# A planner's price for a step of attention is raised, and chunks of the last two batches have one tile each

## The chip, the cores and the metric

The kernel runs on one core of a Trainium2 chip. The metric is the device time of one execution in microseconds (us), as the median of several runs. The core has a matrix engine (TensorE; PE in the profile, PEld for its weight loads), VectorE (DVE), ScalarE (ACT), GpSimd (POOL) and a queue for transfers (SyncE, SP). Each engine works off its own list of instructions in order.

## The reference, cut to what matters

```python
# q, k, v: (batch 8, heads 8, sequence 576, head_dim 64), float32
scores = scale * np.matmul(q, k.transpose(0, 1, 3, 2))
kth = np.partition(scores, -32, axis=-1)[..., -32:-31]     # the 32nd largest of a row
scores = np.where(scores >= kth, scores, -1e9)
attn = softmax(scores)                                      # exp(s - max) / (sum + 1e-9)
x = np.matmul(attn, v)                                      # then (B*S, H*D) = (4608, 512)

h = x @ w_in                                                # w_in: (512, 2048)
g = np.where(h >= 1, h, np.where(h <= -1, 0, (h + 1) ** 2 / 4))
out = g @ w_out                                             # w_out: (2048, 512)
```

Attention keeps only the 32 largest scores of each row, and a feed-forward block (the MLP) follows on the same tokens.

## The kernel before, in words

**Steps of attention.** A batch's 576 queries are cut into four tiles of 128 and a tail of 64. The tails of two batches share one tile of tokens. A step takes one tile of queries for two heads (or half of a tail's heads); there are 144 steps, numbered from 0. In a step TensorE multiplies queries and keys (`scores`, L269), ScalarE copies the scores to `s` (L271), VectorE finds the 32 largest of each row by rounds of eight (L279 to L324: maximum of pairs, maxima, replacement) and masks the exponentials (L330), its reciprocal of their sum is L336, GpSimd normalizes (L343), and the weights are transposed, either by TensorE (`transpose_w`, L357) or, in most steps, through DRAM (`move_w`: a ScalarE copy at L372 and two transfers). Then TensorE multiplies the weights and the values (`values`, L389), and ScalarE copies the result into `xT` (L402), which holds the tokens for the MLP.

**The MLP.** It works on chunks of one or two tiles of 128 tokens. For each of 16 blocks of the hidden layer, `hidden` makes four matmuls into `ph` (L419) over all columns of the chunk at once; ScalarE forms `r` and `g` from it (L423, L431), and GpSimd finishes `g` (L436 to L438). `final` multiplies `g` by `w_out` into `py` (L444), one tile at a time, four blocks behind `hidden` (`LAG = 4`). `ph` has two buffers, shared with the values of attention. So a pair of tiles shares the weight loads of L419 and the instructions on ScalarE and GpSimd, while a single tile can start as soon as that tile's attention is done. A unit in the planner is a 128-column part of this work; a tile has 64 units of `hidden` and 64 of `final`.

**What sets the order.** The order on the four compute engines is written out while the program is built (`manual_schedule`). Each step is walked in seven slots; after each slot `advance` hands out MLP products that are ready. It keeps two model clocks. `dve_time` is VectorE's: a step adds `K_TIME`, and `PIECE_TIME` for each piece of weights that is converted in it. `pe_time` is TensorE's: scores add 1.15, values 1.25, a unit of MLP work `UNIT_TIME` = 0.218. A product is handed out only while `pe_time` is below the slot's time `now` on VectorE's clock, and only while its share `due` of the remaining work lasts. What is left after the last step is worked off at the end. `K_TIME` thus says how long a step is, and so how much MLP work fits beside it. `chunks` (L462 to L470) says which tiles go together: single tiles in the first two batches, pairs after that, and in the last two batches two pairs, the shared tail, and four single tiles.

The start, in which weights are converted from 64-bit words (`early`), lasts for the first steps; the change doesn't touch it.

Of the kernel before, what the change touches and what calls it, by code (L numbers as in the profile page):

```python
# [24 lines left out]
def kernel(  # L25
# [131 lines left out]
    def run(ctx, paired):  # L157
# [304 lines left out]
        rounds, chunks = [], []  # L462
        for b in range(0, B, 2):
            a, c, tl = [(b, t) for t in range(NT)], [(b + 1, t) for t in range(NT)], (b, NT)
            if b + 2 < B:
                rounds += a + [tl] + c + [(b + 1, NT)]
                chunks += [a[0:2], a[2:4], c[0:2], c[2:4], [tl]] if b else [[x] for x in a + c + [tl]]
            else:
                rounds += a + [tl, (b + 1, NT)] + c
                chunks += [a[0:2], a[2:4], [tl]] + [[x] for x in c]  # L470
        steps = []
        for b, t in rounds:
            tile_of = (b, t) if t < NT else (b - b % 2, t)
# [36 lines left out]
                inspected += 1  # L510


        K_TIME, PIECE_TIME, UNIT_TIME, SLOTS, EARLY_STEPS, EARLY_SHARE = 10.2, 0.55, 0.218, 7, 4, 32
        pe_time, dve_time, done, scored, ready_at, usable = 9.0, 12.0, {}, {}, {}, {0: 0.0}

        def advance(amount, until):
# [172 lines left out]
    with ExitStack() as inner:  # L689
        run(inner, True)  # L690
    again = nc.values_load(flag[0:1, 0:1], min_val=0, max_val=1)
    with tc.If(again > 0):
        with ExitStack() as inner:
            run(inner, False)
# [27 lines left out]
```

## Time and profile before

The time is 1684.64 us (median of 3 runs, 1683.96 to 1685.89); the profiled execution took 1683.5 us.

| engine | busy us | share of the span |
|---|---|---|
| PE | 1549.2 | 92% |
| PEld | 1050.8 | 62% |
| DVE | 1550.5 | 92% |
| ACT | 1188.2 | 71% |
| POOL | 974.8 | 58% |

The costliest groups are the output products (L444, 564.3 us busy) and the hidden products (L419, 594.1 us) on TensorE, and the replacement and maxima (L306, 375.6 us; L315, 348.9 us) on VectorE. Busy shares are means over the whole span, so they are to be read together with the rows by slice, which show when an engine was busy. TensorE's busy time counts a matmul from its start to a modelled end, and matmuls overlap. A row of the timeline or of the groups names the line, the engine, the operation, what is written and what is read, and in brackets the idle time before and what ended it.

### The profile page before, as it was taken

Reading aid. Unit: us, or ns where it says so; the run is one execution under the profiler, and the core shown is the slowest. Engines: PE = TensorE matmul, PEld = TensorE weight load, DVE = VectorE, ACT = ScalarE, POOL = GpSimd, SP = SyncE. Lnnn points to the kernel's source line nnn. Section 1 sums busy time; section 2 is a strip of 40 time slices with the busy share of each in tenths; the row PEclk is TensorE's granted clock in tenths of the full one; section 3 lists DMA queues with packets and bytes.
Section 4 is the critical chain, followed back from the end, with each engine's and each line's share of the span. In section 5 each row is a group of like instructions: output and inputs, shape, how many; then the busy total and the mean of one; then the engine's idle time right before and its main releaser. Section 6 shows DMA issues by size and latency. Waiting matters only on the chain.

```text
span 1683.5 us, 30910 instructions
## 1 busy us (share of the span) xinstructions
PE 1549.2 (92%) x9645; PEld 1050.8 (62%) x9645; DVE 1550.5 (92%) x4875; ACT 1188.2 (71%) x2552; POOL 974.8 (58%) x1720
## 2 busy tenths in 40 slices
PE   5586999999998899979999999979999999999998
PEld 4464666666665666646566766646566666666675
DVE  6999999999999999999999999999999999999922
ACT  5677677777777767777677877767667877767743
POOL 4675677666665554536465755526465765657750
PEclk6698999999998999979999999979999999999999
DMA  9333345455555546554555555554555544544400
GB/s 246 114 98 91 86 132 160 129 151 141 140 154 156 144 135 174 142 157 135 146 159 143 150 142 151 158 158 124 155 150 151 143 131 130 132 133 117 114 27 16
DMA packets 439055, 227.83 MB, mean 135 GB/s; under 512 B 393056, under 2 KB 401248, under 8 KB 438880
## 3 DMA queue, kind: packets, MB, share of 16 engines
q1 hardware_dynamic: 438880, 225.75, 49.4%
q8 instruction: 78, 1.28, 0.3%
q14 instruction: 97, 0.79, 0.2%
HBM read 62.91 MB, written 86.11 MB: 89 GB/s over the span
## 4 chain that ended last, share of the span: by engine, by line
DVE 51%; PE 33%; ACT 7%; issue 3%; POOL 3%; DMA 2%; SPq 1%; DVEq 0%; POOLq 0%; ACTq 0%
PE ph L419 13%; DVE more L306 12%; PE py L444 12%; DVE tops L315 10%; DVE e L330 8%; DVE more L317 4%; DVE seconds L320 4%; DVE tops L290 4%; DVE more L279 4%; PE po L389 3%; PE sp L269 3%; ACT halves L372 2%; ACT e L293 1%; DVE z L335 1%; DVE kth L324 1%
## 5 line engine op out<-in xcount | busy, mean ns | idle before, releaser
L419 PEld LDWEIGHTS ph<-xT,w_in 128*128 128x128 f32 x3328 | 505.1, 195 | 199.0 <-issue 88.5
L419 PE MATMUL ph<-xT,w_in 128*128 128x128 f32 (+1 forms) x3328 | 594.1, 326 | 32.8 <-ACT g L431 18.6
L444 PE MATMUL py<-w_out,g 128*128 128x512 f32 x1152 | 564.3, 605 | 2.0 <-POOL w_out L136 1.8
L423 ACT ACTIVATE r<-ph,half 128x128 f32<-128x128 f32 (+1 forms) x416 | 169.7, 408 | 292.9 <-PE ph L419 237.6
L306 DVE MATCH_REPLACE8 more<-tops,more 128x288 f32<-128x288 f32 x864 | 375.6, 442 | 0.0
L436 POOL TENSOR_SCALAR r<-r 128x128 f32<-128x128 f32 (+1 forms) x392 | 164.9, 421 | 343.4 <-ACT r L423 342.1
L315 DVE MAX8 tops<-more 128x8 f32<-128x288 f32 x864 | 348.9, 445 | 0.0
L343 POOL TENSOR_SCALAR e<-e,rz 128x576 f32<-128x576 f32 x260 | 211.9, 825 | 205.2 <-DVE rz L336 205.2
L372 ACT COPY halves<-e 128x1152 uint16<-128x1152 uint16 x260 | 286.9, 1156 | 14.7 <-POOL e L343 14.0
L444 PEld LDWEIGHTS py<-w_out,g 128*128 128x128 f32 x1152 | 197.4, 191 | 145.9 <-issue 117.8
L438 POOL TENSOR_TENSOR g<-r,g 128x128 f32<-128x128 f32 (+1 forms) x400 | 261.6, 654 | 31.4
L330 DVE SCALAR_TENSOR_TENSOR e<-s,kth,e 128x576 f32<-128x576 f32 x288 | 242.0, 877 | 0.5
L437 POOL TENSOR_TENSOR r<-r 128x128 f32<-128x128 f32 (+1 forms) x392 | 219.0, 559 | 32.7
L293 ACT ACTIVATE e<-s,nmax 128x576 f32<-128x576 f32 x288 | 218.4, 771 | 4.8
L269 PE MATMUL sp<-kT,qT 64*128 64x288 f32 x1024 | 169.0, 447 | 9.9 <-ACT kT L229 9.1
L271 ACT ACTIVATE s<-sp 128x576 f32<-128x576 f32 x288 | 170.0, 642 | 6.6 <-PE sp L269 6.4
L389 PE MATMUL po<-wT,v_in 128*64 128x128 f32 x2048 | 148.5, 287 | 22.1 <-DMA wT<-rows 13.9
L389 PEld LDWEIGHTS po<-wT,v_in 128*64 128x64 f32 x2048 | 115.5, 141 | 80.7 <-issue 18.3
L431 ACT ACTIVATE g<-ph,minus 128x128 f32<-128x128 f32 (+1 forms) x400 | 162.4, 406 | 0.0
L269 PEld LDWEIGHTS sp<-kT,qT 64*128 64x128 f32 x1024 | 91.8, 193 | 84.6 <-issue 40.6
L320 DVE MAX8 seconds<-more 128x8 f32<-128x288 f32 x288 | 118.3, 452 | 13.9
L317 DVE TENSOR_TENSOR more<-s 128x576 f32<-128x576 f32 x144 | 122.4, 850 | 4.9
(88 smaller groups left out, 1349.6 us busy)
## 6 DMA issues: line engine op xcount, KB each, us to landing
rows<-halves SPq DMA_DIRECT2D x130, 576.0 KB, 2.8
raw<-in_moe_w_out_dram SPq DMA_DIRECT2D x52, 256.0 KB, 3.0
raw<-in_moe_w_in_dram SPq DMA_DIRECT2D x48, 256.0 KB, 3.1
k_in<-in_k_dram SPq DMA_DIRECT2D x64, 128.0 KB, 2.9
q_in<-in_q_dram SPq DMA_DIRECT2D x32, 256.0 KB, 3.1
v_in<-in_v_dram SPq DMA_DIRECT2D x8, 1024.0 KB, 6.0
out_dram<-y SPq DMA_DIRECT2D x32, 256.0 KB, 2.6
kT<-in_moe_w_in_dram SPq DMA_DIRECT2D x16, 256.0 KB, 4.5
```

What stands on the lines that cost most here:

```text
L269: nc.tensor.matmul(o[:, a0 - c0:a1 - c0], qT[d, g, :], kT[d, g, k0:k0 + a1 - a0], start=True, stop=True)
L293: nc.scalar.activation(e[:, i, :], s[:, i, :], AF.Exp, bias=nmax[:, i:i + 1])
L306: nc.vector.match_replace(out=rest[:, i, :], in_to_replace=tops[:, i, r - 8:r], in_values=src[:, i, :], imm_value=LOWEST)
L315: nc.vector.max(out=tops[:, i, r:r + 8], in_=src[:, i, :])
L330: nc.vector.scalar_tensor_tensor(out=e[:, i, :], in0=s[:, i, :], scalar=last[:, i:i + 1], in1=e[:, i, :], op0=ALU.is_ge, op1=ALU.mult, acc ...
L343: nc.gpsimd.tensor_scalar(e[:, i, :], e[:, i, :], rz[:, i:i + 1], 1.0, ALU.mult, ALU.mult)
L372: nc.scalar.copy(halves[:, :, i * S:(i + 1) * S], st["e"][:, i, :].bitcast(U16).rearrange("p (k t) -> p t k", t=2))
L389: nc.tensor.matmul(po[j * D:(j + 1) * D], v_in[:, h, c, :] if c < NT else v_tl[0][:, h, :], wT[:, block(j, c)], start=(c == 0), stop=(c == ...
L419: nc.tensor.matmul(ph, w_in[:, kk, f * P:(f + 1) * P], xT[:, kk, c0:c1], start=(kk == 0), stop=(kk == NK - 1))
L437: nc.gpsimd.tensor_tensor(out=r, in0=r, in1=r, op=ALU.mult)
L438: nc.gpsimd.tensor_tensor(out=g, in0=r, in1=g, op=ALU.add)
L444: nc.tensor.matmul(pys[i], gs[f][:, i * P:(i + 1) * P], w_out[:, f, :], start=(f == 0), stop=(f == NF - 1))
```

## The change

`K_TIME` goes from 10.2 to 10.7 us, so that the planner takes an attention step to be longer and hands out more MLP products beside each. In the last two batches each chunk has one tile, so that a tile's MLP can begin without waiting for a second tile. The work that is computed is the same.

```diff
@@ -467,7 +467,7 @@
                 chunks += [a[0:2], a[2:4], c[0:2], c[2:4], [tl]] if b else [[x] for x in a + c + [tl]]
             else:
                 rounds += a + [tl, (b + 1, NT)] + c
-                chunks += [a[0:2], a[2:4], [tl]] + [[x] for x in c]
+                chunks += [[x] for x in a + [tl] + c]
         steps = []
         for b, t in rounds:
             tile_of = (b, t) if t < NT else (b - b % 2, t)
@@ -510,7 +510,7 @@
-        K_TIME, PIECE_TIME, UNIT_TIME, SLOTS, EARLY_STEPS, EARLY_SHARE = 10.2, 0.55, 0.218, 7, 4, 32
+        K_TIME, PIECE_TIME, UNIT_TIME, SLOTS, EARLY_STEPS, EARLY_SHARE = 10.7, 0.55, 0.218, 7, 4, 32
         pe_time, dve_time, done, scored, ready_at, usable = 9.0, 12.0, {}, {}, {}, {0: 0.0}
```

## The prediction

> **What bounds the kernel now.** I read the slices of the span first, then the chain, then the busy time by stretch.
>
> ```profile
> PE   5586999999998899979999999979999999999998
> DVE  6999999999999999999999999999999999999922
> PEclk6698999999998999979999999979999999999999
> ...
> DVE 51%; PE 33%; ACT 7%; issue 3%; POOL 3%; DMA 2%; SPq 1%; DVEq 0%; POOLq 0%; ACTq 0%
> ```
>
> VectorE works at 9 tenths until the last two slices, some 80 us in which TensorE alone works off MLP products; TensorE is at 9 tenths nearly everywhere, and the chain hops between the two. So two engines are full, and a "free" 80 us tail must be read against that. The next answer gives busy time by stretch from the end of step 107 (1219 us) on; a row is its window, then its length, then PE, PEld, DVE, ACT, POOL busy, clock, DMA share, GB/s.
>
> ```profile
> 1219.00:1489.00 270.00, 269.21 (x1646) 179.00 (x1645) 262.29 (x828) 197.46 (x399) 162.72 (x268) 0.99 0.52 141
> 1489.00:1542.00 53.00, 48.38 (x312) 34.33 (x310) 51.49 (x163) 37.01 (x83) 33.81 (x69) 0.94 0.41 115
> 1542.00:1607.00 65.00, 64.17 (x458) 45.84 (x460) 61.98 (x194) 47.28 (x115) 48.00 (x101) 1.00 0.41 114
> 1607.00:1684.00 77.00, 69.16 (x417) 49.45 (x411) 10.99 (x40) 26.70 (x81) 20.55 (x55) 0.97 0.04 12
> ```
>
> TensorE idles 0.8, 4.6 and 0.8 us of these 388 us. Since busy time can hide stalls, I priced TensorE's blocks from its timeline, start to start of the next block, at the first quartile of each kind: one-tile hidden product of four matmuls 0.89 us, two-tile one 1.73, output product 0.86, scores of a step 2 x 0.58, values of a step 1.24, a query or key transposition 0.44. The tail shows two of them bare (1642.35 to 1643.21 and to 1644.10):
>
> ```profile
> 1642.35 1.02 PE L444 MATMUL py<-w_out,g 128*128 128x512 f32 x2
> 1643.21 1.05 PE L419 MATMUL ph<-xT,w_in 128*128 128x128 f32 x8
> 1644.10 4.46 PE L444 MATMUL py<-w_out,g 128*128 128x512 f32 x10
> ```
>
> Priced so, 1219 to 1489 holds 260.4 us of work in 270.4 (lost 10.1), 1489 to 1542 holds 42.5 in 53.3 (lost 10.9), 1542 to 1607.5 holds 64.2 in 65.5 (lost 1.3), and the tail to TensorE's last matmul at 1677 holds 66.4 in 67.6 (lost 1.1). In all 433.5 us of work and 23.4 lost; then 6.5 us for the last copy and store. **Everything this change can win after step 107 lies in those 23.4 us.** Part of the loss is VectorE's pace: the second half of a step's scores (L271) lands 4.8 to 6 us before the maximum of pairs (L279) takes it in most steps from 112 to 135. After step 136 this lead is 0.0 to 2.3 us: there TensorE sets the pace already. At the start of a one-tile chunk the loss is of another kind:
>
> ```profile
> 1538.38 2.99 PE L419 MATMUL ph<-xT,w_in 128*128 128x128 f32 x24
> 1542.84 1.16 PE L419 MATMUL ph<-xT,w_in 128*128 128x128 f32 x8 [1.46 <-ACT g L431]
> ```
>
> Hidden products without output products between them (LAG is 4) wait for ScalarE to empty `ph`, which has two buffers.
>
> **What the Trainium skill says.** "Perfetto Trace Analysis", section Identifying the Most-Contended Engine, says that matmul busy share doesn't tell how close TensorE is to its limit; the trace agrees (323 to 456 us: 127 us busy by the profile, 120.1 us of priced work), hence my pricing. "VectorE: DVE Perf Modes", section on the TRN2 errata, gives a ScalarE instruction from PSUM a fixed part of 172 cycles plus one per element at 1.2 GHz: 250 and 357 ns for 128 and 256 columns. The trace has 367 and 473 (L423): the slope agrees, the fixed part is 117 ns larger, and the measurement counts. So halving a chunk pays the fixed part twice. "TensorE: Matmul & The Clock Gate", section What's actually happening, says that after an idle window of about 3.4 us the array runs at half clock. The trace agrees: after gaps of 2.13 and 0.95 us near 1497 us the clock is halved from 1498.7 to 1505.5 us (16 records in 3.78 us, against 1.95 at 1490).
>
> **The change, part by part.** The planner runs while the program is built, so its bookkeeping for both kernels can be counted. A unit is a 128-column quarter of a tile's hidden or output product; a tile has 128.
>
> *K_TIME 10.7.* VectorE's real step is 10.36 us at best and 10.8 on the mean after step 107; so the model now lets TensorE's model clock run 0.5 us further, some 2 units a step. Until step 77 the count at the ends of steps is equal, but for 4 to 16 units early in steps 11 to 22, where `due` or missing tiles bind instead. After step 107 both have 3080 handed out; at the last step before has 4340 and after 4420. The tail's backlog falls from 268 to 188 units: 80 x 0.2188 us (an eighth of 0.89 + 0.86) = 17.5 us less tail. But these 80 units aren't gone. They are put into steps 108 to 143, ahead of scores and values in TensorE's queue. What waits behind them is scores L269, then ScalarE L271, then VectorE L279. The lead of 4.8 us absorbs the first units; after that VectorE pays. With 37.4 units a step in place of 35, priced work is 37.4 x 0.2188 + 1.16 + 1.24 = 10.6 us, plus 0.2 for transpositions: 10.8, before any loss. TensorE becomes the bound of all of these steps, so the end follows from its work and its loss.
>
> *One-tile chunks.* Two pairs become four tiles. TensorE: 32 x (2 x 0.891 - 1.727) = 1.8 us more. The rows by shape:
>
> ```profile
> L423 ACT ACTIVATE r<-ph,half 128x128 f32<-128x128 f32 x256 | 94.0, 367 | 140.7 <-PE ph L419 85.7 <-POOL g L438 41.2 <-POOL r L437 5.9
> L431 ACT ACTIVATE g<-ph,minus 128x128 f32<-128x128 f32 x240 | 87.4, 364 | 0.0
> L423 ACT ACTIVATE r<-ph,half 128x256 f32<-128x256 f32 x160 | 75.6, 473 | 152.2 <-PE ph L419 151.9
> L431 ACT ACTIVATE g<-ph,minus 128x256 f32<-128x256 f32 x160 | 75.0, 469 | 0.0
> ```
>
> ScalarE: 32 x (2 x 731 - 942) ns = 16.6 us more. GpSimd, likewise from L436 to L438 (383 + 457 + 544 against 476 + 706 + 819 ns): 24.5 us more. Both lie beside other work, as ScalarE has 27% idle from 1219 to 1489 and GpSimd 40%. What isn't beside other work is the start of a chunk: nine one-tile chunks now begin between steps 113 and 143, where there were four and two pairs. Starts cost TensorE 0.8, 2.4, 0.8 and 1.7 us late (near 1297, 1494, 1524, 1540 us) and about 2.4, 2.3 and 1.8 us early (359, 403, 452). Bounds 0.8 and 2.4; I take 1.45, the mean of the late four: 13 us. Between starts the one-tile stretches lose 2% (1542 to 1607) up to 5% (323 to 456, less its starts); I take 2.5% of about 320 us: 8. The pair stretch to step 113 keeps its 2, and the tail its 1.1. Sum 24.1 us lost on 435.3 of work, against 23.4 on 433.5: +2.5 us. The gain of readiness (no dry spell near step 124) is in that: with 10.7 and pairs alone the planner would leave 204, with both 188.
>
> *Steps 78 to 97.* Of the same backlog up to 24 more units are out by step 88 (2544 against 2520), yet both run dry at 2816 at step 97. The lead at steps 81 to 86 is 0.0 to 2.1 us already; 12 to 24 units are 2.6 to 5.2 us, so VectorE is delayed by 1 to 4 us. It works back to back afterwards and can't make it up: +3.
>
> *Steps 11 to 22.* Up to 16 units come earlier while TensorE still idles (90 of 113 us busy from 78 to 191): 0 to 2 us gained, I take 1.
>
> Sum: +2.5 + 3 - 1 = +4.5 us, or 1689 us.
>
> **The rivals.** *A, the forecast: TensorE bound, the tail's gain spent in the steps, 1689.* *B: the backlog pays.* If TensorE, never short of work, loses only the 2 to 2.5% of its best stretch, 435.3 x 0.025 = 11 us are lost, 12 fewer than now; against 1.8 for the smaller products and 2 for steps 78 to 97: 1676. For it: that stretch is fed as all steps will be (lag of 12 units, no lead, 38 units a step in 11.2 us). Against it: it is 65 us long, with one start, no key transpositions. *C: no change, 1684.6:* gains of feeding (9 us less from the waits and half clock near 1497) and the new starts cancel. *D: one-tile chunks are as bad as early.* From 323 to 456 us, also one-tile and without lead, 13.4 of 133.5 us are lost; 10% over 320 us is 32, plus 4 elsewhere: 36 against 23.4, plus 1.8 and 3: 1702. Against it: its chunks come just in time, and hidden products wait for `xT` (0.47 us near 360); with a backlog of over 40 units they don't.
>
> **How the numbers follow.** A 0.44, B 0.27, C 0.19, D 0.10. A's bounds (starts at 0.8 or at 2.4 us) run from 1683 to 1698, so a little of it falls within 0.2%, balanced by C's spread. The range from 1674 to 1700 takes in B's centre and leaves out about 2 in 10, most of D and the best of B. Faster by over 0.2% is B: 0.27; within it 0.22; slower 0.51.
>
> **What would show it.** VectorE's last reciprocal (L336), now 1607.5 us, should come near 1629, with 17 us less after it; the mean step from 107 on should grow from 10.8 to about 11.3 us, with VectorE's idle before L279 (10.7 us in all now) at 20 or more; ScalarE's x128 row (L423) should grow by 64, its mean unchanged; hidden products should wait more for ScalarE's `g` L431 (45.9 us on weight loads now). If the steps stay at 10.8 us while the tail shrinks by 17, B is right and my loss at chunk starts is wrong; if idle before L279 stays under 12 us the claim that TensorE becomes the bound falls. If the delay shows already at step 97, the part on steps 78 to 97 is right.

## The result, and the profile after

The changed kernel takes 1700.53 us (median of 4 runs), the kernel before 1684.39 us: ratio 1.0091, 95% interval 1.0074 to 1.0109. It is slower by 16 us, where the prediction had 4.5 us; that is the very end of its range (1674 to 1700 us).

The slices of the span of the changed kernel:

```profile
PE   5586999999998999979899999979999999999998
DVE  6999999999999999999999999999999988899852
PEclk6698999999998999979999999979999999999999
```

Its chain of waits, by engine:

```profile
PE 51%; DVE 33%; ACT 8%; POOL 4%; issue 3%; DMA 1%; SPq 0%; POOLq 0%; DVEq 0%; ACTq 0%
```

VectorE, at 9 tenths up to the tail before, now shows eights in slices 33 to 35 and 38, and works on into slice 39. The chain has changed hands, from 51% on VectorE to 51% on TensorE. The next two lines are the stretch from VectorE's reciprocal of step 107 to its last one, and the tail, in the columns of the prediction:

```profile
1224.50:1635.70 411.20, 399.70 (x2734) 277.12 (x2733) 376.02 (x1185) 296.73 (x675) 286.91 (x557) 0.99 0.47 127
1635.70:1698.60 62.90, 55.75 (x354) 39.91 (x352) 10.79 (x37) 21.50 (x63) 11.31 (x30) 0.99 0.03 11
```

The tail has shrunk, from 76.0 to 62.9 us. But the 36 steps ahead of it have grown from 388.5 to 411.2 us, while VectorE is busy in them for 376 us, as before. Where VectorE waits is told by the idle time before the maximum of pairs:

```profile
L279 DVE TENSOR_TENSOR more<-s 128x576 f32<-128x576 f32 x144 | 113.8, 790 | 32.6 <-ACT s L271 32.5
```

It was 10.7 us in the whole span before, and 1.2 us of that came after step 107; now 24.0 us come after step 107. This accounts for the whole growth of these steps: 22.8 us more idle for 22.7 us. The lead of the scores shows the same: before, the second half of a step's scores was in `s` 4.8 to 6 us ahead of the maximum of pairs in most steps from 112 to 135; now the lead is 0.0 to 1.5 us in every step from 115 on. The longest of these waits is this one, in step 140 (the timeline of VectorE):

```profile
1592.19 0.44 DVE L306 MATCH_REPLACE8 more<-tops,more 128x288 f32<-128x288 f32 x1
1598.31 0.76 DVE L279 TENSOR_TENSOR more<-s 128x576 f32<-128x576 f32 x1 [5.68 <-ACT s L271]
```

And this is TensorE meanwhile, at the start of a one-tile chunk. The first two lines are the row of five hidden products (eight records each) with which a chunk begins:

```profile
1581.92 3.99 PE L419 MATMUL ph<-xT,w_in 128*128 128x128 f32 x32
1586.14 1.16 PE L419 MATMUL ph<-xT,w_in 128*128 128x128 f32 x8 [0.23 <-ACT g L431]
1587.14 1.02 PE L444 MATMUL py<-w_out,g 128*128 128x512 f32 x2
1590.11 1.34 PE L419 MATMUL ph<-xT,w_in 128*128 128x128 f32 x8 [1.95 <-ACT g L431]
1591.25 1.91 PE L444 MATMUL py<-w_out,g 128*128 128x512 f32 x2
1592.95 1.73 PE L419 MATMUL ph<-xT,w_in 128*128 128x128 f32 x8
1594.61 1.24 PE L269 MATMUL sp<-kT,qT 64*128 64x288 f32 x8
```

A hidden product waits 1.95 us for ScalarE to empty `ph`; the scores that VectorE needs stand behind it in TensorE's list. The gap costs more than its length: the granted clock is halved from 1590.95 to 1594.36 us, and the hidden product at 1592.95 takes 1.73 us instead of 1.05. The waits of ScalarE in the same microseconds lead one engine further:

```profile
1585.46 0.37 ACT L423 ACTIVATE r<-ph,half 128x128 f32<-128x128 f32 x1 [0.77 <-POOL g L438]
...
1589.43 0.37 ACT L423 ACTIVATE r<-ph,half 128x128 f32<-128x128 f32 x1 [3.34 <-POOL g L438]
```

ScalarE has no buffer of `r` until GpSimd has finished an earlier block (`r` has two), and GpSimd stood at its normalization (L343) and what follows; some of its instructions were slow there too (L436 took 0.86 us at 1587.5, 0.29 us at 1590.7), for which no run gives the cause. So the chain of this longest wait is GpSimd, `r`, ScalarE, `ph`, TensorE, scores, VectorE.

### The profile page after: what moved, and what is told of

It is laid out like the page before. It is cut to its first block, busy times and chain, and to the rows that moved or that the text cites. A ratio compares the mean times of both kernels' runs of the same rounds, so it can differ in the third digit from the quotient of the medians.

```text
span 1698.6 us, 31644 instructions
## 1 busy us (share of the span) xinstructions
PE 1557.9 (92%) x9901; PEld 1060.4 (62%) x9901; DVE 1557.0 (92%) x4875; ACT 1198.3 (71%) x2616; POOL 1015.4 (60%) x1816
## 4 chain that ended last, share of the span: by engine, by line
PE 51%; DVE 33%; ACT 8%; POOL 4%; issue 3%; DMA 1%; SPq 0%; POOLq 0%; DVEq 0%; ACTq 0%
PE ph L419 19%; PE py L444 19%; DVE more L306 8%; DVE tops L315 7%; PE sp L269 5%; DVE e L330 5%; PE po L389 5%; DVE more L317 3%; DVE seconds L320 3%; DVE tops L290 2%; DVE more L279 2%; ACT halves L372 2%; ACT e L293 1%; POOL g L438 1%; DVE bits L132 1%
## 5 line engine op out<-in xcount | busy, mean ns | idle before, releaser
L419 PEld LDWEIGHTS ph<-xT,w_in 128*128 128x128 f32 x3584 | 519.0, 194 | 205.6 <-issue 95.9
L419 PE MATMUL ph<-xT,w_in 128*128 128x128 f32 (+1 forms) x3584 | 601.5, 314 | 36.9 <-ACT g L431 25.9
L436 POOL TENSOR_SCALAR r<-r 128x128 f32<-128x128 f32 (+1 forms) x424 | 175.8, 415 | 373.4 <-ACT r L423 372.7
L423 ACT ACTIVATE r<-ph,half 128x128 f32<-128x128 f32 (+1 forms) x448 | 178.2, 398 | 296.2 <-PE ph L419 248.0
L343 POOL TENSOR_SCALAR e<-e,rz 128x576 f32<-128x576 f32 x260 | 223.6, 871 | 146.8 <-DVE rz L336 146.8
L437 POOL TENSOR_TENSOR r<-r 128x128 f32<-128x128 f32 (+1 forms) x424 | 231.8, 547 | 35.4
L431 ACT ACTIVATE g<-ph,minus 128x128 f32<-128x128 f32 (+1 forms) x432 | 171.1, 396 | 0.0
L279 DVE TENSOR_TENSOR more<-s 128x576 f32<-128x576 f32 x144 | 113.8, 790 | 32.6 <-ACT s L271 32.5
```

What stands on the lines that cost most here:

```text
L343: nc.gpsimd.tensor_scalar(e[:, i, :], e[:, i, :], rz[:, i:i + 1], 1.0, ALU.mult, ALU.mult)
L419: nc.tensor.matmul(ph, w_in[:, kk, f * P:(f + 1) * P], xT[:, kk, c0:c1], start=(kk == 0), stop=(kk == NK - 1))
L437: nc.gpsimd.tensor_tensor(out=r, in0=r, in1=r, op=ALU.mult)
```

## The experiments

All ratios are to the kernel before on the same chip; the times in us come from several chips, so small differences are to be read from the ratios.

| kernel | us | ratio, 95% interval |
|---|---|---|
| changed kernel | 1700.5 | 1.0091 (1.0074 to 1.0109) |
| 10.7, old chunks | 1689.5 | 1.0044 (1.0025 to 1.0062) |
| 10.2, one-tile chunks | 1688.3 | 1.0026 (1.0019 to 1.0033) |
| 10.7 from step 107, old chunks | 1686.9 | 1.0014 (1.0005 to 1.0023) |
| changed, turns from step 107 | 1684.3 | 1.0000 (0.9990 to 1.0009) |
| changed, turns in all steps | 1675.0 | 0.9949 (0.9933 to 0.9966) |
| before, turns in all steps | 1671.8 | 0.9925 (0.9899 to 0.9950) |
| 10.2, one-tile chunks, turns in all steps | 1671.0 | 0.9923 (0.9906 to 0.9939) |
| 10.7 from step 107, old chunks, turns in all steps | 1668.8 | 0.9916 (0.9891 to 0.9940) |
| changed, `ph` in halves | 1766.7 | 1.0510 (1.0477 to 1.0542) |
| changed, `ph` and `r` in halves | 1750.7 | 1.0398 (1.0369 to 1.0427) |
| changed, LAG 2 | 1723.6 | 1.0237 (1.0220 to 1.0254) |
| changed, LAG 6 | 1739.3 | 1.0333 (1.0316 to 1.0350) |

**The two parts alone.** One run has `K_TIME` 10.7 with the old chunks, one the new chunks with 10.2.

> K_TIME 10.7 with the old chunks. Theory (TensorE bound; delays from two places): VectorE's last reciprocal of step 107 is 5.5 us later than in the kernel before, as in the changed kernel, and the steps after it lose little more, since the pairs stay: 1686 to 1692 us. Rival 1 (more work per step is the whole harm, the chunks none): 1698 or more. Rival 2 (the chunks are the whole harm): 1684 or less.

> One-tile chunks with K_TIME 10.2. Theory: nothing moves up to step 107; after it 1.8 us more work on TensorE and starts of chunks that cost some 1.5 us each, five more of them: 1689 to 1695 us. Rival 1 (work per step is the whole harm): 1684.4. Rival 2 (the chunks are the whole harm): 1698 or more.

Both parts harm, neither is the whole of it: +0.44% and +0.26%. Both single-cause rivals fall. 1689.5 us is within what was expected of 10.7; 1688.3 us is just under the range expected of the chunks. The sum, 0.70%, is below the 0.91% of both together; with intervals of up to 0.18% on either side that difference may be chance. In the profiles the idle before L279 after step 107 is 1.2 us in the kernel before, 8.5 us with 10.7 alone, 4.5 us with the chunks alone, and 24.0 us with both. The leads of the scores suggest why: with 10.2 most steps leave TensorE time to make up for a start, with 10.7 they don't.

**When the longer step costs.**

```diff
-                dve_time = start + K_TIME + PIECE_TIME * min(len(now_converting), n_pieces - converted)
+                dve_time = start + K_TIME + (0.5 if m >= 107 else 0.0) + PIECE_TIME * min(len(now_converting), n_pieces - converted)
```

> Old chunks, and 10.7 only from step 107 on. Theory: the 5.5 us of delay at step 107 are not there, and the rest is as with 10.7 throughout: 5 to 6 us under that run, 1681 to 1687 us. Rival (the harm of 10.7 lies in the steps after 107): within 1.5 us of that run.

1686.9 us is at the upper end of what was expected. It is 2.6 us under 10.7 throughout by the medians and 0.30%, some 5 us, by the ratios, whose intervals just part (1.0023 and 1.0025): a delay before step 107 is there, and is worth a sixth to a third of the whole loss. It can be seen between the reciprocals of steps 77 and 107: 321.4, 321.0 and 321.0 us in the three kernels with 10.2 there (the one before, new chunks alone, 10.7 late), and 326.1, 325.5 and 323.6 in those with 10.7 (the changed kernel, 10.7 alone, the turns below). The last three have the same order of work up to there, so what they differ by is chance.

But VectorE hardly waits for TensorE in these steps. Between the reciprocals of steps 77 and 97 its idle before L279 grows by 0.6 us only, while its own instructions take 3.8 us longer. The stretch before and after (columns as in the prediction; VectorE is the third engine, GpSimd the fifth):

```profile
897.80:1112.70 214.90, 210.28 (x1256) 138.54 (x1254) 208.34 (x660) 161.89 (x329) 121.91 (x207) 0.99 0.57 154
898.60:1118.00 219.40, 212.69 (x1256) 138.24 (x1254) 212.18 (x662) 161.79 (x329) 127.44 (x207) 0.99 0.55 149
```

VectorE is busy for 207.5 to 208.5 us there in all six kernels of the table with 10.2 in these steps. It is busy for 210.4 to 212.2 us in four with 10.7: the changed kernel, 10.7 with the old chunks, and the changed kernel with either kind of turns. The longer ones are L279, L317, L321 and L335 (L335, on two columns, 4.56 us in all before and 6.05 after); on GpSimd L343 and L345 lengthen in the same steps (30.5 to 33.6 and 4.4 to 6.5 us). So the planner's hand-out shifts which instructions of VectorE and GpSimd run beside each other; that they slow each other would fit, but no run isolates it.

What is left of 10.7 after step 107, 0.14%, is the shorter tail (59.1 us from the last reciprocal to the end of TensorE's work, 69.5 before) against longer steps (400.6 us, 388.5 before; 9 us of that is idle before L279 and 3 us longer instructions of VectorE): even with pairs the handed-out work was paid for in full.

**Turns: a start without a row of hidden products.** The last four output products of a chunk alternate with the first four hidden products of the next. Nothing is left out or computed differently, only the order changes.

```diff
-                    pending.extend(mlp(xTs[ch], chunks[ch], mlp_pool, ch == len(chunks) - 1))
+                    work = mlp(xTs[ch], chunks[ch], mlp_pool, ch == len(chunks) - 1)
+                    if valued > 106 and len(pending) >= LAG:
+                        ends = [pending.pop() for _ in range(LAG)][::-1]
+                        work[0:LAG] = [x for two in zip(ends, work[0:LAG]) for x in two]
+                    pending.extend(work)
```

> The changed kernel, but from step 107 on the last four output products of a chunk are handed out in turn with the first four hidden products of the next chunk, so that a start has no row of five hidden products. Theory (starts of one-tile chunks cost TensorE 1 to 2 us each): 8 to 12 us faster than the changed kernel, 1689 to 1693 us, and the waits of 12 to 16 us steps are gone. Rival (one-tile instructions slow ScalarE and GpSimd everywhere): within 3 us of the changed kernel, 1698 to 1701.

1684.3 us: the gain is 16 us, more than the 8 to 12 expected, and the loss is gone. In the profiles 1.8 us of it stand before step 107, where the order of work is the same, and are chance; the steps after 107 are 14 us shorter. Priced by block as in the prediction, TensorE's steps after 107 hold 380.0 us of work and 29.9 lost in the changed kernel, 382.9 and 15.6 with turns. In the stretches from 3 us before to 15 us after the nine starts, 18.7 us are lost without turns and 7.6 with them. The longest idle before L279 fell from 5.68 to 2.6 us. ScalarE and GpSimd do the same one-tile instructions there, and are as busy (ScalarE 296.3 us after step 107, 296.7 without turns; GpSimd 287.0 and 286.9), so the size of the instructions alone isn't what costs. The waits from step 107 to the last reciprocal, of the changed kernel and then with turns:

```profile
DVE more L279 <- ACT s L271: 24.0, 15, 5.7
PEld ph L419 <- ACT g L431: 17.4, 21, 2.8
ACT r L423 <- POOL g L438: 14.6, 9, 3.3
```

```profile
DVE more L279 <- ACT s L271: 10.2, 11, 2.6
PEld ph L419 <- ACT g L431: 7.7, 12, 1.7
ACT r L423 <- POOL r L437: 3.0, 3, 1.1
```

Less than half is left of the first two, and of ScalarE's 14.6 us for GpSimd's `g` 2.7 us.

**Turns everywhere** (the condition on step 106 dropped), with the old and the new chunks and all three ways to set `K_TIME`:

> The kernel before with chunk ends and starts handed out in turn in all steps, also in the first two batches, where starts cost 2 us each. Theory: 4 to 10 us faster than the kernel before, 1674 to 1680 us. Rival (VectorE sets the pace with 10.2, starts are hidden): 1684 within 2.

> Old chunks, 10.7 from step 107 on, and ends and starts in turn everywhere. Theory: without start losses the longer steps cost less than the tail wins, so it is under the kernel with turns and 10.2 by 1 to 5 us. Rival (TensorE's work is conserved, nothing to win by handing out more): the same within 2 us, or slower.

> The changed kernel with ends and starts handed out in turn in all steps. Theory: the turns win 10 to 13 us more in the first batches, as they did for the kernel before, so 1671 to 1675 us, near the old chunks with turns. Rival (one-tile chunks cost 5 us or more in themselves): 1678 or more.

> The same with K_TIME 10.2. Theory: without the delay of steps 77 to 107, and without start losses, 3 to 5 us under the same with 10.7: 1667 to 1671 us. Rival (the larger backlog at the end decides): above the same with 10.7.

The kernel before gains 13 us, more than expected: 8.7 of them up to step 107 (1219.0 to 1210.3 us), most of the rest after. VectorE's idle before L279 falls from 10.7 to 1.9 us. The changed kernel with turns everywhere is at the upper end of its expected range, and so is the run with 10.2 and one-tile chunks. The chunks, with turns and 10.2, are neutral (1671.0 against 1671.8): the rival that one-tile chunks cost 5 us in themselves falls. `K_TIME` 10.7 throughout costs 4 us more than 10.2 even then, though the intervals still overlap a little (0.9933 and 0.9939), and 10.7 from step 107 has the lowest median, 1668.8 us, 16 us under the kernel before; its 3 us over turns with 10.2 lie within the intervals (0.9891 to 0.9940 against 0.9899 to 0.9950), so only the turns are shown to pay.

**More room in `ph`.** One-tile chunks use half of a buffer, so two blocks were put into one.

```diff
+                shared = len(tiles) == 1 and f % 2
+                if not shared:
+                    both["ph"] = ps.tile([P, CW], F32, name="ph", tag="ph", bufs=2)
+                ph = both["ph"][:, c1 - c0:2 * (c1 - c0)] if shared else both["ph"][:, 0:c1 - c0]
```

> The changed kernel, but in a one-tile chunk two hidden blocks share one buffer of ph, half each, so that up to four blocks can be under way in place of two. Theory (TensorE waits at starts since ScalarE empties two buffers too slowly): 4 to 10 us faster than the changed kernel, 1690 to 1696. Rival (ScalarE is itself held up, by the two buffers of r that GpSimd must free): within 3 us of the changed kernel, 1698 or more.

> The same, and r shared in halves too. Theory (ph alone counts): within 2 us of the run with halves of ph. Rival (the buffers of r hold ScalarE up): 4 us or more faster than that run, and the waits of ScalarE's r L423 for GpSimd are gone.

The first did the opposite of what it was made for, 66 us slower. In its trace the first matmul of an odd block starts only after ScalarE has read the even half in all 152 cases (one-tile chunks without the last); in the changed kernel it does so in 39 of 152. The Trainium skill ("PSUM — Partial Sum Buffer", section PSUM bank collisions raise a hardware error) says that two engines must not be in the same bank at once, even at different addresses; a wait between the halves keeps to that. So this is a run with the suspected wait nearly tripled rather than removed, and it answers in that sense. It does so for the one-tile chunks of the first batches too: 29 us against the changed kernel are lost by step 107. The waits of the matmuls themselves for `ph`, in the changed kernel and in this one (whose lines stand three further down):

```profile
PE ph L419 <- ACT g L431: 25.9, 33, 1.9
```

```profile
PE ph L422 <- ACT g L434: 72.3, 71, 3.6
```

VectorE's idle before L279 rises with it, from 32.5 to 86.6 us. With `r` in halves too 16 us come back. `r` isn't in PSUM, and no such wait shows: in 77 of 152 odd blocks ScalarE writes its half before GpSimd is done with the even one. VectorE's idle falls to 72.8 us, and ScalarE's wait for `g` on GpSimd falls from 28.1 to 8.2 us. My theory had `ph` alone count; the rival is right that the two buffers of `r` hold ScalarE up as well. Four separate buffers of `ph` were not tried, so the relief itself isn't shown.

**The length of the row.** `LAG` sets how many hidden products stand in a row at a start, in all steps; the buffers of `g` stay at eight.

> The changed kernel with output products two blocks behind the hidden ones instead of four (buffers of g as before), so that a chunk's start has a row of three hidden products instead of five. Theory (the length of the row is what costs): 5 to 12 us faster than the changed kernel in steps 107 to 143, and some gain in the first two batches: 1680 to 1694 us. Rival (any cost of a start is the switch of chunks itself, not the row): 1698 to 1703; slower still if two blocks are too few for GpSimd to finish g.

> The same with six blocks: rows of seven hidden products at a start, and six output products at an end. Theory: 8 us or more slower than the changed kernel, 1708 or more. Rival (the switch itself): within 3 us of the changed kernel.

Six blocks cost 39 us, in the direction expected and more of it. Two blocks were expected to win and cost 23 us, as the rival had it for a `g` that isn't finished in time: the waits of matmuls for `ph` did shrink, but output products now wait for GpSimd's `g`. The first two lines are from LAG 2, the line after them from the changed kernel:

```profile
PE py L444 <- POOL g L438: 44.2, 48, 2.6
...
PE ph L419 <- ACT g L431: 5.4, 9, 1.5
```

```profile
PE py L444 <- POOL g L438: 0.8, 2, 0.7
```

So a short row cures the start and starves the steady part: four lies between two waits (three and five were not run), and turns escape both. ScalarE never waits for a buffer of `g` in the three kernels, so the eight buffers aren't what six blocks run into. As LAG acts everywhere, these two runs support the mechanism but don't size it for the late steps.

## Why the prediction was right in direction and short in size

The profile reads as steps of a sum; the span grew by 15.1 us (1683.5 to 1698.6).

- *TensorE becomes the bound and the tail's gain is spent in the steps.* Right, and the core of it. The last reciprocal was forecast near 1629 us and came at 1635.7; the mean step after 107 was to be about 11.3 us and is 11.4; idle before L279 was to exceed 20 us and was 32.5.
- *A tail 17.5 us shorter.* It is 13.1. The hidden and output products behind the last reciprocal fell from 71 to 52, 16.6 us at 0.875, but three blocks of values stand behind it instead of one, and two groups of weight transpositions instead of one: TensorE lags more, so attention work slid into the tail.
- *1.8 us more work for one-tile products.* Right: priced work after step 107 went from 433.4 to 435.3 us.
- *Loss of 24.1 us after step 107 in place of 23.4.* Too small: 30.0, 5.9 us more than forecast. Of this, 18.7 us lie in the stretches around the nine starts, small stalls included: 2.1 us a start where 1.45 had been taken (13 in all). The other 11 are what had been taken for everything else. So the mis-sized term is the cost of a start. Two readings made it low. Among the four late starts stood a stall near 1524 us in the middle of a chunk (that chunk began at 1490), while the start at 1577 us was left out, which lost 1.2 us in the same measure. And only 2.4 us were counted for the start at 1490 us; with the further stalls and the matmuls at half clock, it lost 7.0 us.
- *Steps 78 to 97: +3.* The place was right and the size near it, 4.5 us by step 97 here (2.5 to 5.0 up to step 107 in the three runs with 10.7 over the mean of the three with 10.2). The path was wrong: VectorE was to be held up by scores that come late, but its wait for them grew by 0.6 us and its own instructions by 3.8. The number was luck.
- *Steps 11 to 22: -1.* Not seen. Step 22 ends 0.9 us later and step 77 0.8 us later; at step 77 runs with the same order of work lie up to 3 us apart. The units came earlier, but TensorE was already behind: the scores of steps 15 and 18 arrive as VectorE takes them in both kernels.

The terms in sum: 0.8 + 4.7 up to step 107, 1.9 of work, 6.6 of loss over the kernel before: 14.0 of 15.1; the rest sits at the edges of the stretches. So 1700.5 us lies outside the forecast's own bounds (1683 to 1698) and next to rival D (1702), which had been given 0.10. D isn't what happened either: its rate of loss, 10% of the late one-tile steps, was not reached (29.9 of 409.9 us is 7.3%), and its total loss of 36 us is as far off as the 24.1 of the forecast. In terms of loss, work and steps before 107, the forecast was 0.7 + 1.8 + 2, D was 12.6 + 1.8 + 3, and the runs show 6.6 + 1.9 + 5.5. The mechanism held after step 107; before it, it did not.

The prediction also took the half clock near 1497 us to agree with the idle window of about 3.4 us that it cites. The gaps there are 2.13 and 0.95 us, and in the changed kernel one of 1.95 us was followed by half clock, so no whole window of idleness was needed.

Readiness of single tiles, the purpose of the new chunks, was not worth its price. After step 107 the planner's backlog never ran empty in the kernel before either (by the order of the matmuls, 41 units stand open at the end of step 124 and 16 at the least). With 10.7 and pairs it did, from 1415 to 1420 us, and a gap of 1.93 us follows near 1423; single tiles remove that, and yet 10.7 with pairs is the faster kernel (1689.5 against 1700.5 us).

## What to carry to other kernels

Where two engines are both near full, a long tail on one of them is not idle time to be filled: work moved ahead of it is paid for where it lands, and if it stands in front of what the other engine needs, with interest. Look for the stalls in the full engine instead, by pricing its blocks from their best spacing in the trace; here that showed chunk starts, and a change of order alone took 13 us off. Before making pieces finer, see what happens at the seam between two pieces, for there will be more seams.

## What the runs showed that was not expected

- Two halves of a PSUM tile are not two buffers here: writer and reader took turns in all 152 cases, 66 us for a change that was meant to double the buffers.
- Changing `LAG` by two either way, with no other work, costs 23 and 39 us.
- In the kernel before most of the gain from turns comes early, where chunks have one tile from the outset: 4.9 us by step 22 and 8.7 by step 107, without any change in what is computed.
- Handing out more MLP work made instructions of VectorE itself longer, 3.8 us in 20 steps, though it waited no more.
